# A planned attention and expert kernel: one attention pair joined at the start, one visit joined at the end, two constants of the planner changed

## The chip, the cores and the metric

The kernel runs on one core of a Trainium2 chip. The metric is device time in microseconds (us), from the start of an execution to its end. Before the change it takes 629.05 us, the median of three runs (628.59 to 629.12).

The core has five engines that matter here. TensorE (PE in the profile) multiplies matrices and writes to PSUM, which has eight banks. VectorE (DVE), ScalarE (ACT) and GpSimd (POOL) do elementwise work[...]. SyncE (SP) issues nearly all DMAs. Each engine takes its own instructions in order and waits on semaphores for the others.

## The reference

The first stage is a gated linear attention (4 sequences, 8 heads, 768 positions, head width 32, state width 16), taken in chunks. The second stage sends its result, as 3072 tokens of 256 numbers, through four expert layers and mixes them. All numbers are float32.

```python
for c in range(nc):                     # attention, chunk by chunk
    cum = np.cumsum(log_a[:, :, sl], axis=-1)
    M = einsum('bhin,bhjn->bhij', Cc, Bc) * exp(cum_i - cum_j) * causal
    y = einsum('bhij,bhjd->bhid', M, xc) + einsum('bhin,bhnd->bhid', Cc, state) * exp(cum)
    state = exp(sum(la)) * state + einsum('bhjn,bhjd->bhnd', Bc * exp(cum_last - cum), xc)
...
p = domain_probs / (domain_probs.sum(-1, keepdims=True) + 1e-09)
for e in range(E):                      # four experts, F = 1024
    h = np.maximum(x @ w1[e], 0.0)
    out += p[:, e:e + 1] * (h @ w2[e])
```

## The kernel before

**Tiling.** The kernel uses chunks of 128 positions, so there are 24 chunks: four sequences of six. The chunks are numbered so that the first four begin the four sequences and need no state from earlier. They are grouped in five blocks, of 4, 4, 4, 6 and 6 chunks, and a pair of chunks is 256 tokens. For the first three blocks (scheme B) and the last two (scheme H) the expert layers are computed with fast matrix multiplication: 7 products in place of 8 in scheme B, 15 in place of 18 in scheme H. The price is many sums of weights (L963), of tokens (L982), of hidden values (`combine`, L901) and of results (L1180). One product is two float32 matmuls of 128 x 128 by 128 x 256 (L874), and each of these shows as two records in the profile.

**Attention of a pair.** For each chunk, `decays` scans the decays into a buffer LT on VectorE (L496), makes a small product on GpSimd (`fade`, L506, into the buffer MT), and masks a copy of C on ScalarE (`mask`, L472). A visit of TensorE that computes scores (`score`, L479) fills four banks, and VectorE multiplies each with LT into MT (L798). A second visit (`outputs`) applies the state (L820, for chunks after the first four) and MT (L512, `inner`), and ScalarE copies the result out (L835), and the new state where there is a later chunk (L522). These visits use small tiles of the array, placed by `tile_position`. There are two MT buffers and one LT buffer.

**Opening.** Chunks 0 and 1 are written out by hand, up to 13.2 us. Chunks 2 and 3 come next, in `line`, TensorE's fixed order: the spreading of chunk 2's decays (L627), then scores and outputs of each chunk singly, with the first products of block 0 (`first`) between them. `beside` (L85) gives chunk 3 a second Value on the same LT and MT buffers, so that the planner sees no dependence between the two chunks there.

**The planner.** The program makes no schedule by hand after that. `Plan.add` records every job with the engines that may take it, its estimated time, what it needs and what it writes. `Plan.run` then plays the engines against each other and writes the instructions out in the order found. TensorE follows `line`. Every other engine takes, of the jobs that are ready and for which buffers are free, the one that is due first (`latest`). Three rules touch the change:

- A job that both VectorE and GpSimd may do (`B512`, `B256`: L901 without a PSUM operand, L963 for scheme B, L1180 without PSUM) is taken by GpSimd only if it will end in time there, and if VectorE has more urgent work that is ready, worth at least `BACK` us. The 100 sums of L963 for scheme H are for GpSimd alone.

```python
if max(ready, now) + w.on[e] > w.latest + late + SLACK or self.backlog(
        waiting["DVE"], now, t["DVE"], w) < BACK:
    continue
```

- Work on any engine but SyncE counts on the data of a load `MARGIN` us after the planned landing; the same holds for a buffer whose last user was a DMA.
- `PAIRS_AT` says, for a block of so many units followed by one of so many pairs, at which unit and place of `line` the next block's scores ("s0") and outputs ("o1", "o12") are visited. A unit is one group of fast products, some 26 us long (23 units in about 600 us). The key (6, 3) is that of block 3, in which the last block's attention is done.

Of the kernel before, what the change touches and what calls it, by code (L numbers as in the profile page):

```python
# [20 lines left out]
LANDING = 2.2  # L21
KEEP = 5
NV, NW = 31, 28
SLACK, BACK, YIELD = 0.0, 1.0, 6.0
EARLY = 1, 2, 3, 4, 5, 6, 7, 8, 9, 10
SOFT = 1
ROUND = 0, 3, 2, 0, 4
RATE, MARGIN = 330.0, 4.0
AFTER = 1
HOLD = 12.0  # L30
NEAR, WORTH, FIRST = .3, 1.0, 25.0
WAIT = .15
LANES, ISSUE = 8, .48
URGENT = {}
HELD = ("x", "w"), (5, 8), (0, 7)
LAST = (0, 1), (0, 2), (1, 1), (1, 2), (0, 0), (1, 0)
LATE = (13, 2), (6, 9), (11, 4), (10, 12), (3,), (1, 14), ("x", "w"), (5, 8), (0, 7)
# [6 lines left out]
}  # L44


# [5 lines left out]
class Value:  # L52
    def __init__(self, kind, seeded=False, fills=True):
        self.kind, self.seeded, self.fills = kind, seeded, fills
        self.home, self.writers, self.readers, self.left, self.end = None, [], [], 0, 0.0
        self.keeps = self.before = None

    @property
    def t(self):
# [12 lines left out]
class Plan:  # L72
# [9 lines left out]
        v.end = v.ready = ready  # L82
        return v

    def beside(self, v):  # L85

        u = Value(f"{v.kind} beside")
        u.home, u.end, u.ready = v.home, v.end, v.ready
        self.spare[u.kind] = []
        u.keeps = v  # L90
        return u

    def add(self, on, fn, reads=(), writes=(), part=(), lag=None, due=None, reuse=None, two=False,
            port=True, after=None, kb=0, hold=0.0, pieces=1):
        w = Work(on, fn, (.16 if "PE" in on else .09) if lag is None else lag)
        w.hold = hold
        w.two, w.port, w.after, w.kb, w.pieces = two, port, after, kb, pieces
        w.due, w.reuse = due, reuse
        w.ready = 0.0
        for v in reads:  # L100
            w.needs.update(v.writers)
            w.ready = max(w.ready, getattr(v, "ready", 0.0))
            v.readers.append(w)
        for v in writes:
            w.needs.update(v.writers)
            w.needs.update(v.readers)
            v.writers, v.readers = [w], []
        for v in part:
            w.needs.update(v.readers)
            v.writers = v.writers + [w]  # L110
        w.needs.discard(w)
        keeps = [v.keeps for v in (*reads, *writes, *part) if v.keeps]
        for v in dict.fromkeys([*reads, *writes, *part, *keeps]):
            w.touched.append(v)
            v.left += 1
        for n in w.needs:
            n.feeds.append(w)
        w.number = len(self.all)
        self.all.append(w)
        return w  # L120
# [222 lines left out]
def kernel(  # L343
# [15 lines left out]
    NSEQ = NCH // NC  # L359
# [65 lines left out]
    st = {c: {} for c in range(NCH)}  # L425
# [210 lines left out]
    LT, MT = ([homes[k][0][:, c] for c in range(2)] for k in ("LT", "MT"))  # L636
# [52 lines left out]
    ys = []  # L689
# [13 lines left out]
    plan = Plan(homes)  # L703
    line = []
    B512, B256 = {"DVE": D512, "POOL": 1.3}, {"DVE": D256, "POOL": .72}
    now = 13.2

    def pe(us, fn, **kw):
        w = plan.add({"PE": us}, fn, **kw)
        line.append(w)  # L710
        return w
# [22 lines left out]
        st[c]["xb"] = plan.taken("xb", i, now)  # L734
    st[2]["ctm"] = plan.taken("ctm", 0, now)
    st[3]["ab"] = plan.taken("ab", 0, now + 2)
    for k, i in (("LT", 0), ("MT", 1)):
        st[2][k] = plan.taken(k, i, now)
        st[3][k] = plan.beside(st[2][k])
    for c in range(2):  # L740
        st[c]["A"] = plan.taken("A", c, now)
    g0 = gates[0, 0] = plan.taken("gate", 0, now)
# [15 lines left out]
    def decays(c):  # L758
        s = st[c]
        j = c % 2  # L760
        for k in ("LT", "MT") if not j and "MT" not in s else ():
            s[k] = st[c + 1][k] = value(k)
        for part in range(2):
            if c < SPREAD:
                dve(1.2, lambda e, part=part: scan_quarters(
                    c, s["LT"].t[:, j], [b.t for b in s["a"]], part), reads=s["a"][2 * part:2 * part + 2],
                    part=[s["LT"]])
            else:
                half = NH * P // 2
                dve(1.15, lambda e, lo=half * part: scan(  # L770
                    s["LT"].t[:, j], s["ab"].t[:, lo:lo + half], place(c, lo // P) * P), two=True, reads=[s["ab"]], part=[s["LT"]])
        if c < NCH - NSEQ:
            plan.add({"POOL": .5 if place(c, 0) else .4}, lambda e: fade(c, s["MT"].t[:, j], s["xb"].t, s["LT"].t[:, j]),
                     reads=[s["xb"], s["LT"]], part=[s["MT"]])
        if "ctm" not in s:
            s["ctm"] = value("ctm")
            act(.62, lambda e: mask(c, s["ctm"].t, s["xb"].t), reads=[s["xb"]], writes=[s["ctm"]])
        if c >= NSEQ:
            s["dec"], s["cts"] = value("dec"), value("cts")
            dve(D256, lambda e: nc.vector.tensor_tensor_scan(  # L780
                out=s["dec"].t, data0=s["ah"].t, data1=zeros, initial=1.0,
                op0=ALU.mult, op1=ALU.add), two=True, reads=[s["ah"]], writes=[s["dec"]])
            plan.add({"POOL": .72}, lambda e: nc.gpsimd.tensor_mul(  # L783
                s["cts"].t, s["ctm"].t, s["dec"].t.unsqueeze(1).to_broadcast([HN, NT, P])),
                reads=[s["ctm"], s["dec"]], writes=[s["cts"]])

    def scores(cs):
        gs_ = [value("bank", fills=len(cs) == 2) for _ in range(NQ)]
        ss = [st[c] for c in cs]
        pe(.66 * len(cs), lambda e: score(  # L790
            cs, [s["ctm"].t for s in ss], [s["xb"].t for s in ss], [b.t for b in gs_]),
            reads=[s[k] for s in ss for k in ("ctm", "xb")], writes=gs_)
        s = ss[0]
        for r in (3, 2, 0, 1):
            def fn(e, r=r):
                g = gs_[r].t.rearrange("p (c t s) -> p c t s", c=2, t=NT)[:, :len(cs)]
                js, h = slice(cs[0] % 2, cs[0] % 2 + len(cs)), quarter(cs[0], r)
                nc.vector.tensor_mul(s["MT"].t[:, js, h, 0:P], g, s["LT"].t[:, js, h])  # L798

            dve(D512 if len(cs) > 1 else D256, fn, reads=[gs_[r], s["LT"]], part=[s["MT"]], hold=HOLD)  # L800
# [5 lines left out]
    def outputs(cs):  # L806
        ys = {c: value("bank", fills=False) for c in cs}
        for c in cs:
            if pair_of(c) not in yT:
                yT[pair_of(c)] = value("V")  # L810
        reads = [st[c][k] for c in cs for k in ("xb", "MT", "cts") if k in st[c]]
        reads += [S[c - NSEQ] for c in cs if c >= NSEQ]

        def fn(e):
            vs = {}
            for c in cs:
                vs[c] = v = ys[c].t[:, :NT * (P + N)].rearrange("p (t s) -> p t s", t=NT)
                for r in range(NQ) if c >= NSEQ else ():
                    rows, to = slice(32 * r, 32 * r + 32), 32 * ((r + turn_of(c)) % NQ)
                    nc.tensor.matmul(  # L820
                        out=v[to:to + 32, :, 0:P], lhsT=S[c - NSEQ].t[rows],
                        rhs=st[c]["cts"].t[rows], start=True, stop=False,
                        tile_position=(32 * r, to), skip_group_check=True)
            for c in cs:
                for t in range(NT):
                    inner(c, t, vs[c][:, t], st[c]["xb"].t, st[c]["MT"].t[:, c % 2],
                          P + N if c < NCH - NSEQ else P, c < NSEQ and t == 0)

        pe(.93 + .49 * len(cs) if cs[0] >= NSEQ else .75 * len(cs), fn, reads=reads, writes=list(ys.values()))
        for c in cs:  # L830
            s, y = st[c], ys[c]
            yt = yT[pair_of(c)]
            v = lambda y: y.t[:, :NT * (P + N)].rearrange("p (t s) -> p t s", t=NT)
            lo = c % 2 * P
            act(.28, lambda e, y=y, yt=yt, lo=lo: nc.scalar.copy(  # L835
                out=yt.t[:, :, lo:lo + P], in_=v(y)[:, :, 0:P]), reads=[y], part=[yt])
            if c < NCH - NSEQ:
                s["A"] = value("A")
                act((.1, .4, .2, .4)[turn_of(c)], lambda e, c=c, s=s, y=y: keep_state(
                    c, s["A"].t, v(y)[:, :, P:]), reads=[y], part=[s["A"]])  # L840
# [433 lines left out]
    fbs = range(EPB)  # L1274
# [11 lines left out]
    for fb in fbs:  # L1286
        first[fb, 0], h[fb, 0] = plain_first(0, fb, 0)
    decays(2)
    line.extend(first[0, 0])
    scores([2])  # L1290
    line.extend(first[1, 0])
    decays(3)
    outputs([2])
    scores([3])
    line.extend(first[2, 0])
    line.extend(first[3, 0])
    outputs([3])
    line.extend(visit(0, (2, 4), plain_terms(0, fbs, h, [(0, 0), (1, 0)])))
    for c in range(4):
        carry(c)  # L1300
# [146 lines left out]
```

## Time and profile before

| | before |
|---|---|
| median of 3 runs | 629.05 us |
| the profiled execution | 628.72 us |
| its span, first to last instruction | 626.9 us |
| granted TensorE clock | 1.000 |
| TensorE matmul / weight loads busy | 620.4 / 529.6 us |
| VectorE busy | 522.7 us, 822 instructions |
| ScalarE busy | 267.6 us, 563 instructions |
| GpSimd busy | 235.6 us, 257 instructions |
| DMA | 125.87 MB, mean 201 GB/s |

Busy time of TensorE is no measure here, since matmuls overlap in the pipeline and their ends are modelled; the distance from one matmul's start to the next one's is. A group's row gives the number of instructions, the time in which any of them ran, the mean of one, and the engine's idle time just before them with what ended it. The chain that ended last is followed back from the last instruction, at each step to what released it.

### The profile page before, as it was taken

What the parts mean: (1) busy time and instruction counts of PE and PEld (TensorE: products, weight loads), DVE (VectorE), ACT (ScalarE), POOL (GpSimd) and SP (SyncE); (2) the same over time, 40 slices, a digit from 0 to 9 for tenths busy, and PEclk for the clock granted to TensorE, in tenths of its full rate; (3) what the DMA queues carried; (4) which work ended last, traced back from release to release, by engine and by line L of the source; (5) the groups of instructions that cost most, each with busy time, mean ns of one, the idle gap of its engine ahead of it and who ended that gap; (6) DMA issues with size and microseconds to landing.
All of it is one profiled execution on the core that took longest, in us unless ns stands there. A gap on an engine that the chain in (4) does not pass through costs nothing.

```text
span 626.9 us, 10322 instructions
## 1 busy us (share of the span) xinstructions
PE 620.4 (99%) x3443; PEld 529.6 (84%) x3443; DVE 522.7 (83%) x822; ACT 267.6 (43%) x563; POOL 235.6 (38%) x257
## 2 busy tenths in 40 slices
PE   9999999999999999999999999999999999999997
PEld 5888888888888888888888888888888888888886
DVE  6989999988857799799779988959796967879684
ACT  4322553434355253246524335355444334554441
POOL 4244555662635756155763413220122310112020
PEclk9999999999999999999999999999999999999999
DMA  7989586673799875799999736636222229643001
GB/s 258 313 282 348 185 273 215 228 236 94 240 331 298 270 227 168 203 349 312 351 326 302 235 96 206 198 112 194 61 88 72 55 61 352 189 140 112 1 1 50
DMA packets 111733, 125.87 MB, mean 201 GB/s; under 512 B 28853, under 2 KB 78273, under 8 KB 111681
## 3 DMA queue, kind: packets, MB, share of 16 engines
q1 hardware_dynamic: 111412, 125.07, 62.6%
q8 instruction: 27, 0.44, 0.3%
q14 instruction: 26, 0.20, 0.1%
q10 hardware_dynamic: 268, 0.16, 0.1%
HBM read 100.30 MB, written 24.89 MB: 200 GB/s over the span
## 4 chain that ended last, share of the span: by engine, by line
PE 91%; DVE 7%; issue 1%; ACT 1%; DVEq 0%; ACTq 0%
PE bank L874 85%; PE bank L479 2%; PE bank L512 2%; DVE v L901 2%; DVE v L909 1%; DVE w L963 1%; DVE LT L496 1%; PE bank L651 1%; PE bank L820 1%; PE bank L627 1%; DVE dec L780 0%; DVE Y L982 0%; DVE MT L798 0%; PE bank L1252 0%; ACT A L522 0%
## 5 line engine op out<-in xcount | busy, mean ns | idle before, releaser
L874 PE MATMUL bank<-v,w 128*128 128x256 f32 x1864 | 438.9, 380 | 0.9 <-DVE v L901 0.7
L874 PEld LDWEIGHTS bank<-v,w 128*128 128x128 f32 x1864 | 352.4, 190 | 54.4 <-issue 3.9
L874 PE MATMUL bank<-Y,w 128*128 128x256 f32 x792 | 203.0, 379 | 0.7 <-ACT bank L888 0.7
L901 DVE TENSOR_TENSOR v<-v,v 128x512 f32<-128x512 f32 x219 | 178.4, 844 | 21.0 <-ACT v L883 19.5
L874 PEld LDWEIGHTS bank<-Y,w 128*128 128x128 f32 x792 | 150.4, 190 | 21.7 <-ACT bank L888 1.1
L901 POOL TENSOR_TENSOR v<-v,v 128x512 f32<-128x512 f32 x51 | 72.1, 1417 | 219.3 <-DVE v L909 124.1
L909 DVE SCALAR_TENSOR_TENSOR v<-bank,gate 128x512 f32<-128x512 f32 x172 | 116.7, 683 | 43.5 <-PE bank L874 39.1
L888 ACT COPY bank<-v 128x512 f32<-128x512 f32 (+1 forms) x192 | 108.3, 576 | 67.7 <-DVE v L901 46.2
L963 POOL TENSOR_TENSOR w<-w,w 128x256 f32<-128x256 f32 x106 | 96.9, 932 | 58.3 <-PE bank L874 35.0
L1129 ACT COPY v<-bank 128x512 f32<-128x512 f32 x107 | 62.6, 585 | 131.4 <-PE bank L874 129.5
L883 ACT COPY v<-bank 128x512 f32<-128x512 f32 x106 | 61.9, 584 | 102.0 <-PE bank L874 92.9
L496 DVE TENSOR_TENSOR_SCAN LT<-ab,ident 128x512 f32<-128x512 f32 x42 | 53.1, 1281 | 0.0
L901 DVE TENSOR_TENSOR v<-bank,v 128x512 f32<-128x512 f32 x40 | 27.4, 685 | 9.6 <-PE bank L874 9.5
L506 POOL TENSOR_TENSOR MT<-xb,LT 128x64 f32<-128x64 f32 (+1 forms) x28 | 15.3, 552 | 35.6 <-DVE LT L496 31.6
L798 DVE TENSOR_TENSOR MT<-bank,LT 128x512 f32<-128x512 f32 (+1 forms) x48 | 27.8, 632 | 0.9 <-PE bank L479 0.8
L1180 POOL TENSOR_TENSOR v<-v,v 128x256 f32<-128x256 f32 x18 | 17.2, 967 | 26.1 <-DVE v L1180 19.8
L783 POOL TENSOR_TENSOR cts<-ctm,dec 128x256 f32<-128x256 f32 x20 | 16.4, 825 | 14.1 <-ACT ctm L472 10.3
L1180 DVE TENSOR_TENSOR v<-v,v 128x256 f32<-128x256 f32 x42 | 17.4, 445 | 4.4 <-ACT v L1129 4.3
L1034 DVE TENSOR_TENSOR bank<-bank,v 128x512 f32<-128x512 f32 x22 | 15.3, 694 | 6.2 <-PE bank L874 6.0
L472 ACT ACTIVATE ctm<-xb,tmask 128x128 f32<-128x128 f32 x48 | 16.4, 395 | 4.1 <-DMA xb<-in_xbc_dram 2.1
L963 DVE TENSOR_TENSOR w<-w,w 128x256 f32<-128x256 f32 x32 | 16.5, 547 | 0.0
L963 POOL TENSOR_TENSOR w<-w 128x256 f32<-128x256 f32 x13 | 12.3, 944 | 10.4 <-PE bank L874 7.4
(72 smaller groups left out, 211.8 us busy)
## 6 DMA issues: line engine op xcount, KB each, us to landing
w<-in_w_dram SPq DMA_DIRECT2D x130, 256.0 KB
w<-w_d SPq DMA_DIRECT2D x130, 256.0 KB
w_d<-w SPq DMA_DIRECT2D x82, 256.0 KB
ab<-acut_d SPq DMA_DIRECT2D x21, 512.0 KB
w<-in_w_dram SPq DMA_DIRECT2D x38, 128.0 KB
gate<-p_d SPq DMA_DIRECT2D x10, 384.0 KB
xb<-in_xbc_dram SPq DMA_DIRECT2D x17, 192.0 KB
gate<-p_d SPq DMA_DIRECT2D x11, 256.0 KB
```

The costliest lines, as they stand in the source:

```text
L472: nc.scalar.mul(ctm[:, t], xb[:, OCT:OCT + P], tmask[:, t:t + 1])
L496: nc.vector.tensor_tensor_scan(out=LT.rearrange("p h s -> p (h s)")[:, lo:lo + w], data0=src, data1=ident.rearrange("p h s -> p (h s)")[:, ...
L783: plan.add({"POOL": .72}, lambda e: nc.gpsimd.tensor_mul(s["cts"].t, s["ctm"].t, s["dec"].t.unsqueeze(1).to_broadcast([HN, NT, P])), reads ...
L798: nc.vector.tensor_mul(s["MT"].t[:, js, h, 0:P], g, s["LT"].t[:, js, h])
L874: nc.tensor.matmul(out=o, lhsT=w[:, j], rhs=x if half is None else x[:, j], start=(start and j == 0), stop=(j == 1), skip_group_check=True)
L883: act(.5, lambda e: nc.scalar.copy(out=flat(v), in_=bank.t), reads=[bank], writes=[v])
L888: act(.54 if to > FB else .32, lambda e: nc.scalar.copy(out=bank.t[:, :to], in_=flat(v)[:, :to]), reads=[v], writes=[bank])
L901: plan.add(engines, lambda e: (on(e).tensor_add if sign > 0 else on(e).tensor_sub)(flat(v), whole(x), whole(y)), reads=[x, y], writes=[v], ...
L909: dve(D512, lambda e: nc.vector.scalar_tensor_tensor(out=h.t, in0=whole(x).rearrange("p (j m) -> p j m", j=JJ), scalar=0.0, in1=g.t[:, 2 * ...
L963: plan.add({"POOL": .72} if due else B256, lambda e, r=r, x=x, y=y, sign=sign: (on(e).tensor_add if sign > 0 else on(e).tensor_sub)(view(r ...
L1129: act(.5, lambda e: nc.scalar.copy(out=flat(v), in_=bank.t), reads=[bank], writes=[v])
L1180: plan.add(engines, lambda e: (on(e).tensor_add if sign > 0 else on(e).tensor_sub)(o[1](), x[1](), y[1]()), reads=[v for v in vs if v is n ...
```

## The change

There are four edits. The third and fourth chunk's scores are computed in one visit and their outputs in one visit; `beside` goes, and both chunks share a Value for LT and one for MT, as later pairs do. `SCORED = 4` puts the scores after the first four products of block 0. In the last block, the outputs of the second and third pair are computed in one visit, at the third pair's place, instead of each at its own. `BACK` goes from 1.0 to 3.0 us, and `MARGIN` from 4.0 to 2.0 us. The estimate of the planner for an outputs visit of the first four chunks is changed along with it.

```diff
-SLACK, BACK, YIELD = 0.0, 1.0, 6.0
+SLACK, BACK, YIELD = 0.0, 3.0, 6.0
...
-RATE, MARGIN = 330.0, 4.0
+RATE, MARGIN = 330.0, 2.0
...
+SCORED = 4
...
-    (6, 3): ((0, 1, "s0"), (0, 14, "o0"), (2, 1, "s1"), (2, 14, "o1"), (3, 1, "s2"), (3, 14, "o2")),
+    (6, 3): ((0, 1, "s0"), (0, 14, "o0"), (2, 1, "s1"), (3, 1, "s2"), (3, 14, "o12")),
...
-    for k, i in (("LT", 0), ("MT", 1)):
-        st[2][k] = plan.taken(k, i, now)
-        st[3][k] = plan.beside(st[2][k])
...
-        for k in ("LT", "MT") if not j and "MT" not in s else ():
+        for k in ("LT", "MT") if not j else ():
...
-        pe(.93 + .49 * len(cs) if cs[0] >= NSEQ else .75 * len(cs), fn, reads=reads, writes=list(ys.values()))
+        pe(.93 + .49 * len(cs) if cs[0] >= NSEQ else .4 + .49 * len(cs), fn, reads=reads, writes=list(ys.values()))
...
     decays(2)
-    line.extend(first[0, 0])
-    scores([2])
-    line.extend(first[1, 0])
     decays(3)
-    outputs([2])
-    scores([3])
-    line.extend(first[2, 0])
-    line.extend(first[3, 0])
-    outputs([3])
+    begun = [x for fb in fbs for x in first[fb, 0]]
+    line.extend(begun[:SCORED])
+    scores([2, 3])
+    line.extend(begun[SCORED:])
+    outputs([2, 3])
```

The rest of the diff removes `beside`, its field `keeps` and the lines in `Plan.add` that served it.

More of the change, by code (lines that the diff above doesn't have):

```diff
@@ L55, in __init__ @@
         self.home, self.writers, self.readers, self.left, self.end = None, [], [], 0, 0.0
-        self.keeps = self.before = None
+        self.before = None
     @property
@@ L83, in taken @@
         return v
[L85 to L91, printed above, removed]
     def add(self, on, fn, reads=(), writes=(), part=(), lag=None, due=None, reuse=None, two=False,
@@ L111, in add @@
         w.needs.discard(w)
-        keeps = [v.keeps for v in (*reads, *writes, *part) if v.keeps]
-        for v in dict.fromkeys([*reads, *writes, *part, *keeps]):
+        for v in dict.fromkeys([*reads, *writes, *part]):
             w.touched.append(v)
```

## The prediction

> **What bounds the kernel now.** I read the page's totals and its chain first, then the chain in order of time, then TensorE's timeline of the opening, then busy time by stage, then the groups. The totals, and the chain's shares by engine:
>
> ```profile
> PE 620.4 (99%) x3443; PEld 529.6 (84%) x3443; DVE 522.7 (83%) x822; ACT 267.6 (43%) x563; POOL 235.6 (38%) x257
> ...
> PE 91%; DVE 7%; issue 1%; ACT 1%; DVEq 0%; ACTq 0%
> ```
>
> TensorE carries 91% of the chain, VectorE 7%. Where these shares change is seen in the chain in order of time (start, us, what):
>
> ```profile
> 59.63 1.07 PE bank L874 x4
> 60.71 0.03 issue
> ...
> 79.45 0.61 DVE v L909
> ...
> 80.14 0.60 ACT bank L888
> 80.74 0.04 issue
> 80.78 16.68 PE bank L874 x76
> ...
> 280.14 0.64 PE bank L820 x32
> 280.79 2.14 PE bank L512 x64
> ...
> 387.77 0.59 PE bank L820 x16
> 388.36 1.01 PE bank L512 x32
> ...
> 418.35 199.63 PE bank L874 x924
> ```
>
> The last line gives TensorE's pace: 199.63 / 924 = 0.216 us from one big matmul to the next. With that pace I went through all 2656 starts of L874: outside the attention visits (L479, L820, L512) the pace breaks only three times, at 79.67 (1.109 us instead of 0.216), 108.30 (0.633) and 299.99 (1.047). That is 0.89 + 0.42 + 0.83, less the 0.10 that a restart costs anyway: 1.9 us of stall in all. Before the first two, the chain has run on VectorE (60.7 to 79.5, and 97.5 to 108.9). The rest of the span is work at full pace, 13.2 us of opening by hand, and about 9 us after the last dense stretch ends at 617.97. So a gain can only come from fewer or cheaper attention visits and from these 1.9 us.
>
> The opening, TensorE's timeline (start, us, engine, line, operation, tiles, shape, count):
>
> ```profile
> 15.13 0.71 PE L479 MATMUL bank<-ctm,xb 32*128 32x256 f32 x8
> 15.77 1.99 PE L874 MATMUL bank<-v,w 128*128 128x256 f32 x8
> 17.70 0.80 PE L512 MATMUL bank<-MT,xb 128*32 128x144 f32 x16
> 18.42 0.71 PE L479 MATMUL bank<-ctm,xb 32*128 32x256 f32 x8
> 19.07 3.72 PE L874 MATMUL bank<-v,w 128*128 128x256 f32 x16
> 22.72 0.70 PE L512 MATMUL bank<-MT,xb 128*32 128x144 f32 x16
> 23.34 14.94 PE L874 MATMUL bank<-v,w 128*128 128x256 f32 x68
> 38.22 1.15 PE L479 MATMUL bank<-ctm,xb 32*128 32x256 f32 x16
> ```
>
> To see here: each of the four visits is short, and a pair's scores (x16, from 38.22 to 39.29) take 1.07 us where two singles take 0.64 + 0.65.
>
> Busy time by stage (stretch, its length, PE, PEld, DVE, ACT, POOL, then clock and DMA):
>
> ```profile
> 50.00:75.00 25.00, 25.00 (x210) 20.98 (x209) 24.69 (x38) 10.11 (x22) 13.10 (x15) 1.00 0.73 249
> ```
>
> The two largest groups that either engine may take (busy us, mean ns, idle before and what ended it):
>
> ```profile
> L901 DVE TENSOR_TENSOR v<-v,v 128x512 f32<-128x512 f32 x219 | 178.4, 844 | 21.0 <-ACT v L883 19.5
> ...
> L901 POOL TENSOR_TENSOR v<-v,v 128x512 f32<-128x512 f32 x51 | 72.1, 1417 | 219.3 <-DVE v L909 124.1
> ```
>
> VectorE is full from about 40 to 110 us (24.69 of 25), and there alone it limits TensorE. In 400 to 425 it is busy 17.89 of 25.
>
> **What the Trainium skill says.** "Perfetto Trace Analysis", Identifying the Most-Contended Engine: matmul busy time is a poor measure of a full TensorE, weight-load time a better one. Agreed: I use start to start (0.216 us) and not the 99%; weight loads stand at 84%. "TensorEngine Tiling (Array Packing)", Key Properties: changing the tiling mode drains TensorE. The trace agrees: the big matmul before a visit takes 0.309 us to the next start, the first after it 0.320, against 0.216: 0.20 us for each visit. "SBUF — State Buffer", Who interferes with whom: an operation of VectorE with two inputs in SBUF and one of GpSimd that reads SBUF shut each other out. The trace agrees: of the 219 operations in the DVE row above, 125 with no GpSimd operation beside them took 683 ns (0.603 from start to start), 94 with one took 1059 ns.
>
> **The change part by part.**
>
> *The opening.* Today: 0.64 + 0.72 + 0.65 + 0.62 us for four visits, and six changes between visit and dense work (two visits adjoin) at 0.10: 3.2 us. After: the paired scores 1.07, paired outputs (32 of L512, 1.05, half of a visit with 64) and four changes: 2.5. That removes 0.7 us, if nothing is late. What may be late is MT on VectorE, which has no idle time there. The third chunk's scans end at 16.23. The fourth chunk's second mask ends at 17.00 on ScalarE; the paired scores come after 16 dense matmuls, at 16.75, and begin with the third chunk's half (0.35 us), so they wait about nothing. VectorE then has the two scans of the fourth chunk (2.33 us), which now share one buffer with the third's and so are planned after its small GpSimd product (16.71); one gate product (0.60) fits in before. Four products of 0.60 follow: 16.23 + 0.60 + 2.33 + 2.40 = 21.56, against 21.48 when TensorE arrives. Stall 0.1; without the gate product, none. The remaining three or four gate products (0.60 each) feed a visit from 22.6 that eats one per 0.43 us; the last is needed at 23.9 and done near 23.5. Gain **0.6 us**, from 0.7 down to 0 if VectorE is one scan later. VectorE itself saves 8 x 0.331 - 4 x 0.60 = 0.25 us. Loads and their queue keep their order here.
>
> *The last block's two pairs in one visit.* One pair costs 389.30 - 387.39 = 1.91 from the last dense start before to the first after, less 0.216 of it, plus 0.10: 1.80 us; two, 3.60. A joint one: 0.64 + 2 x 1.01 + 0.20 = 2.86 (last-block shape; the joint visit at 280.14 took 2.78 with the wider one). Gain **0.7 us**. It needs four free banks at once, and ScalarE copies four tiles out in about 2.0 us instead of 1.0. VectorE is idle a quarter of the time there and the result is used only two units later, so I take nothing off; if banks lack, up to one copy, 0.6 us.
>
> *BACK from 1 to 3.* Jobs that GpSimd may take: on it now 51 of L901, 19 of L1180, and of L963 19 (the code has 64 sums open to both engines, VectorE ran 45). A moved L901 adds 0.60 us to VectorE, a moved half-size one 0.335; each us of GpSimd work that goes relieves VectorE by about 0.20 (the stretching of L901, L963, L780 and L496 beside GpSimd sums to 46 us, over 235.6). If half move: 25 x 0.60 + 19 x 0.335 - 54 x 0.20 = **+10 us of VectorE**, covered by VectorE's idle time after 110 (some 93 of its 104 us); zero on the path. Uncovered it is only in 40 to 110: there at most 2 of L901 and 12 sums, 2 x 0.60 + 12 x 0.335 = 5.2 us if all move and nothing is relieved. From the other side, near 299 two L901 on GpSimd (295.10 and 297.23) stretch a scan to 1.68 and a sum to 1.15 right ahead of the third stall: without them up to 0.8 comes back, and in all at most 1.9. I take **0**.
>
> *MARGIN from 4 to 2.* It removes no work; compute engines are planned up to 2 us sooner after a load. VectorE waited for DMA only in the first 4 us (1.1). GpSimd did wait for loads ("DMA w<-in_w_dram 5.5" in three places), so planned landings are already early when DMA is busy. 2 us more of that on GpSimd is covered (it is idle 62%); on VectorE between 40 and 110 each would cost up to 2. The scores in the opening do not go through it. I take **0**, from -0.5 to +2.
>
> Sum: -0.6 - 0.7 = **-1.3 us** on a span of 626.9: 625.6. That execution took 628.72, 1.8 more than its span; the median is 629.05, so the forecast is 629.05 - 1.3 = **627.7**.
>
> **Rivals.**
>
> 1. *The stalls go as well* (less shutting out by GpSimd): -1.3 and up to -1.9, 625.8 to 626.9. For it: the stretched operations ahead of all three stalls. Against: most GpSimd work at 60 to 110 is sums for later blocks that only GpSimd may do, and it stays.
> 2. *VectorE becomes the bound for longer*: in the gapless stretch from 40 to 110, jobs that GpSimd took with a backlog of 1 to 3 us now queue on VectorE, or VectorE waits for a load. The stalls near 80 and 108 grow by up to 5.2 from the sums, 2 from a load. It decides from 2.6 us of added VectorE time there (1.3 to eat the gain, 1.26 to be seen): 630.3 to 632.9. For it: there is no slack, 0.3 us of idle. Against: relief, and a backlog there may be above 3 anyway.
> 3. *The opening's gain is given back* at 79.7, as VectorE needs the same time to get there: 628.3 to 628.9. Against: it waited for TensorE at 32.3, 34.0 and 39.4 (3.3 us), so an earlier TensorE moves it too.
> 4. *The threshold hardly binds*, GpSimd keeps its share: the same -1.3, within the forecast.
>
> **How the numbers follow.** The forecast, with rival 4, has 0.40 (626.9 to 628.7); rival 1, 0.20; rival 3, 0.08; rival 2, 0.32. A plan is laid anew by two constants, and a list of orders has more ways to get worse than the 1.9 us it can recover, hence the weight of rival 2. 0.2% is 1.26 us, about what a measurement here can tell: faster is below 627.8, slower above 630.3. The forecast's case straddles the first: 0.22 faster, 0.18 same. Faster 0.42, same 0.26, slower 0.32. The range leaves out the lowest quarter of rival 1 and the upper third of rival 2: 626.0 to 631.8; the likeliest case alone is 626.9 to 628.7.
>
> **What would show it.** Right: two visits fewer between 13 and 24, the dense work after them starting at 22.6 to 22.8; one visit with 32 of L820 near 416 and none near 388; GpSimd's L901 about 25; the pace of 0.216 unbroken but near 80, 108 and 300. Wrong: new breaks of pace from 40 to 110 behind VectorE (rival 2), VectorE waiting for a load, or a break at the four-bank visit.

## The result, and the profile after

The changed kernel takes 625.18 us, the median of four runs (624.95 to 625.32), against 629.09 us before in the same session: the ratio is 0.9938, with a 95% interval of 0.9921 to 0.9956. It is 3.9 us faster, where 1.3 us was forecast, and lies below the range of 626.0 to 631.8. The profiled executions took 625.31 us (span 623.5) and 628.72 us (span 626.9), so the two traces differ by 3.4 us, and that is what they can account for. Lines of the changed kernel have other numbers: L874 is now L863, L901 is L890, L909 is L898, L963 is L952, L1180 is L1169, L496 is L488, L798 is L787, L479 is L471, L512 is L504, L820 is L809.

The page after, totals and the chain's shares by engine:

```profile
PE 618.5 (99%) x3443; PEld 530.0 (85%) x3443; DVE 525.2 (84%) x889; ACT 267.7 (43%) x563; POOL 141.8 (23%) x186
...
PE 97%; DVE 1%; issue 1%; ACT 0%; DVEq 0%
```

TensorE's share of the chain rose from 91% to 97%, VectorE's fell from 7% to 1%. GpSimd does 94 us less, and VectorE, which took that work, is busy only 2.5 us longer. The chain in order of time (start, us, what), after:

```profile
16.22 0.58 DVE v L898
16.81 2.25 DVE LT L488 x2
19.05 0.06 DVE v L898
19.11 0.44 issue
19.55 2.49 DVE MT L787 x4
22.04 0.04 issue
22.08 1.18 PE bank L504 x30
...
59.48 11.42 PE bank L863 x52
...
73.66 37.32 PE bank L863 x172
110.98 1.08 PE bank L471 x16
...
281.29 37.32 PE bank L863 x172
...
412.40 0.64 PE bank L809 x32
413.04 1.90 PE bank L504 x64
414.94 199.63 PE bank L863 x924
```

From 73.66 to 110.98, and from 281.29 to 318.61, TensorE runs 172 matmuls without a break; before, these stretches held the breaks at 79.67, 108.30 and 299.99. Near 388 there is no visit any more, and the one at 412 serves both pairs. The opening, TensorE's timeline after:

```profile
16.86 1.15 PE L471 MATMUL bank<-ctm,xb 32*128 32x256 f32 x16
17.93 3.72 PE L863 MATMUL bank<-v,w 128*128 128x256 f32 x16
21.58 1.68 PE L504 MATMUL bank<-MT,xb 128*32 128x144 f32 x32
23.19 14.94 PE L863 MATMUL bank<-v,w 128*128 128x256 f32 x68
```

The outputs visit lasts 1.61 us from start to start instead of the forecast 1.05; the dense work after it starts 0.15 us earlier than before, not 0.6. Taken at equal places of TensorE's order, the 3.40 us lie here:

| where | before | after | won |
|---|---|---|---|
| dense work after the third and fourth chunk's outputs | 23.34 | 23.19 | 0.15 |
| dense work after the scores near 112 (breaks at 79.67, 108.30) | 113.66 | 111.98 | 1.53 |
| dense work after the scores near 320 (break at 299.99) | 322.16 | 319.62 | 0.86 |
| dense work after the last outputs (416 before, 412 after) | 418.27 | 414.87 | 0.86 |

So the two joint visits gave 0.15 + 0.86 = 1.01 us, and the breaks that went 1.53 + 0.86 = 2.39 us. The tail is the same: 8.96 us from 617.97 to the end before, 8.96 from 614.57 after.

For the experiments I use one measure: from the first big matmul's start to the last one's. It leaves out the opening by hand, whose length varies by 0.7 us between profiles. It is 608.28 us before (13.20 to 621.48) and 604.88 after. The breaks before cost 0.89 + 0.42 + 0.83 and, since a restart costs 0.10 more, 2.45 us in all; the changed kernel lost 0.55 us in its opening. Without any loss the old structure would take 605.83 us and the new one 604.33. So 1.50 us are structure and 1.90 us are losses that went away; the 0.55 us that the changed kernel loses in its opening counts against the losses here (2.45 - 0.55), and against the joint visits in the 1.01 above. "Loss" below is what a kernel takes over its structure's figure. It is read from one profiled execution of each kernel, so the ratio beside it, from all executions, counts for more: with BACK = 3.5 the profiled execution (627.38 us) was the fastest of twelve, whose median is 628.56.

### The profile page after: what moved, and what is told of

Read it like the earlier page. It is cut to its first block, busy times and chain, and to the rows that moved or that the text cites. A ratio compares the mean times of both kernels' runs of the same rounds, so it can differ in the third digit from the quotient of the medians.

```text
span 623.5 us, 10234 instructions
## 1 busy us (share of the span) xinstructions
PE 618.5 (99%) x3443; PEld 530.0 (85%) x3443; DVE 525.2 (84%) x889; ACT 267.7 (43%) x563; POOL 141.8 (23%) x186
## 4 chain that ended last, share of the span: by engine, by line
PE 97%; DVE 1%; issue 1%; ACT 0%; DVEq 0%
PE bank L863 91%; PE bank L504 2%; PE bank L471 2%; DVE LT L488 1%; PE bank L643 1%; PE bank L809 1%; PE bank L619 0%; DVE MT L787 0%; PE bank L1241 0%; PE bank L611 0%; ACT A L514 0%; DVE v L898 0%; ACT v L686 0%; DVE v L1169 0%; DVE v L1246 0%
## 5 line engine op out<-in xcount | busy, mean ns | idle before, releaser
L863 PE MATMUL bank<-v,w 128*128 128x256 f32 x1864 | 438.1, 380 | 0.0
L863 PEld LDWEIGHTS bank<-v,w 128*128 128x128 f32 x1864 | 352.5, 190 | 52.5 <-issue 3.1
L863 PE MATMUL bank<-Y,w 128*128 128x256 f32 x792 | 202.9, 379 | 0.0
L890 DVE TENSOR_TENSOR v<-v,v 128x512 f32<-128x512 f32 x261 | 185.2, 740 | 20.3 <-ACT v L872 19.0
L863 PEld LDWEIGHTS bank<-Y,w 128*128 128x128 f32 x792 | 150.4, 190 | 20.6 <-issue 0.2
L898 DVE SCALAR_TENSOR_TENSOR v<-bank,gate 128x512 f32<-128x512 f32 x172 | 116.8, 684 | 35.1 <-PE bank L863 29.6
L952 POOL TENSOR_TENSOR w<-w,w 128x256 f32<-128x256 f32 x94 | 82.5, 899 | 76.2 <-PE bank L863 44.1
L890 POOL TENSOR_TENSOR v<-v,v 128x512 f32<-128x512 f32 x9 | 12.8, 1419 | 236.7 <-DVE v L890 183.3
L488 DVE TENSOR_TENSOR_SCAN LT<-ab,ident 128x512 f32<-128x512 f32 x42 | 51.2, 1228 | 0.0
L890 DVE TENSOR_TENSOR v<-bank,v 128x512 f32<-128x512 f32 x40 | 27.5, 689 | 8.8 <-PE bank L863 8.4
L787 DVE TENSOR_TENSOR MT<-bank,LT 128x512 f32<-128x512 f32 x44 | 27.7, 678 | 0.6 <-PE bank L471 0.6
L1169 DVE TENSOR_TENSOR v<-v,v 128x256 f32<-128x256 f32 x57 | 22.5, 427 | 4.8 <-ACT v L1118 4.7
L498 POOL TENSOR_TENSOR MT<-xb,LT 128x64 f32<-128x64 f32 (+1 forms) x28 | 11.6, 420 | 50.5 <-DVE LT L488 33.1
L464 ACT ACTIVATE ctm<-xb,tmask 128x128 f32<-128x128 f32 x48 | 16.2, 394 | 11.8 <-DMA xb<-in_xbc_dram 10.4
L952 DVE TENSOR_TENSOR w<-w,w 128x256 f32<-128x256 f32 x44 | 18.2, 443 | 0.6 <-issue 0.4
L952 POOL TENSOR_TENSOR w<-w 128x256 f32<-128x256 f32 x12 | 9.5, 792 | 33.1 <-DMA w<-in_w_dram 19.0
L1121 ACT COPY v<-bank 128x256 f32<-128x256 f32 x18 | 6.7, 372 | 19.9 <-PE bank L863 19.7
```

The costliest lines, as they stand in the source:

```text
L464: nc.scalar.mul(ctm[:, t], xb[:, OCT:OCT + P], tmask[:, t:t + 1])
L488: nc.vector.tensor_tensor_scan(out=LT.rearrange("p h s -> p (h s)")[:, lo:lo + w], data0=src, data1=ident.rearrange("p h s -> p (h s)")[:, ...
L863: nc.tensor.matmul(out=o, lhsT=w[:, j], rhs=x if half is None else x[:, j], start=(start and j == 0), stop=(j == 1), skip_group_check=True)
L890: plan.add(engines, lambda e: (on(e).tensor_add if sign > 0 else on(e).tensor_sub)(flat(v), whole(x), whole(y)), reads=[x, y], writes=[v], ...
L898: dve(D512, lambda e: nc.vector.scalar_tensor_tensor(out=h.t, in0=whole(x).rearrange("p (j m) -> p j m", j=JJ), scalar=0.0, in1=g.t[:, 2 * ...
L952: plan.add({"POOL": .72} if due else B256, lambda e, r=r, x=x, y=y, sign=sign: (on(e).tensor_add if sign > 0 else on(e).tensor_sub)(view(r ...
```

## The experiments

**Which constant, and is it the engine or the plan?** The theory after the result was A: jobs that leave GpSimd relieve VectorE, and so the breaks go. Its rivals were B, that MARGIN did it, and C, that breaks are accidents of one plan. Four kernels, on one chip. First BACK alone, in the kernel before:

```diff
-SLACK, BACK, YIELD = 0.0, 1.0, 6.0
+SLACK, BACK, YIELD = 0.0, 3.0, 6.0
```

> The kernel before with BACK = 3 alone. Theory A (less GpSimd work beside VectorE relieves VectorE, and so the three breaks of TensorE's pace go): GpSimd's L901 falls from 51 to about 10, VectorE's busy time rises by less than 5 us, the 2.4 us of breaks (0.89 + 0.42 + 0.83 and 0.10 for each restart) go: about 626.7 us. Theory B (MARGIN did it, since data count sooner): the same shift of jobs, breaks of 2 us or more remain: 629 us or more. Theory C (the breaks are accidents of one plan, and any new plan has others): breaks at new places, 0 to 4 us.

Measured: ratio 0.9992 (0.9984 to 1.0001), no gain that can be told. GpSimd's L901 fell to 9 and VectorE's busy time rose by 7.7 us, yet the loss is still 2.04 us: a break at 79.68 and a wait in the visit near 174.

```diff
-RATE, MARGIN = 330.0, 4.0
+RATE, MARGIN = 330.0, 2.0
```

> The kernel before with MARGIN = 2 alone. Theory A: GpSimd's L901 stays near 51 and breaks of pace of 2 to 3 us remain: 628.5 to 629.5 us. Theory B: the breaks go: about 626.7 us. Theory C: breaks at new places, 0 to 4 us.

Measured: 0.9986 (0.9980 to 0.9993), loss 1.63 us: 627.95 us at the median, where B expected about 626.7, with breaks at 90.5 and 197.4, where none were. A and B both fall as single causes. The next kernel has both structural edits and the constants of before (the changed kernel with the two diffs above taken back):

> The changed kernel with BACK = 1 and MARGIN = 4 as before, so the two structural edits alone. All theories: the joint visit near 416 saves 0.85 us and the opening 0.15, as in the changed kernel. Theory A: breaks of about 2.4 us remain where VectorE is full, so 628.1 us. Theory C: breaks anywhere, 626 to 630.

Measured: 1.0002 (0.9994 to 1.0010). The last outputs visit cost 2.74 us, as in the changed kernel, but there are five breaks (2.49 us in all), four of them where the kernel before has none and one, at 80.29, behind the same matmul as the break at 79.67 before; and the scores of the opening waited. Loss 3.89 us: the structure's 1.50 us are there, and all of it was lost again. Last, the old plan, with only the engine of the shared jobs changed:

```diff
     for w in done:
-        w.fn(w.by)
+        w.fn("DVE" if len(w.on) > 1 else w.by)
```

> The plan of the kernel before, job for job and in the same order, but each of the 89 jobs that it gave to GpSimd and that VectorE may do is written out for VectorE at its place; TensorE's, ScalarE's and SyncE's orders are the same. No new plan is made, so only the engine differs. Theory A: relief nearly pays for the added jobs, VectorE's busy time rises by less than 5 us, breaks of pace fall to 1 us or less: 626.7 to 627.7 us. Theories B and C: VectorE has 89 jobs more than the plan gave it (about 45 us by 0.603 and 0.335 each), breaks grow: 630 us or more.

Measured: 1.0038 (1.0025 to 1.0051). The group of sums on VectorE in this kernel (busy us, mean ns, idle before), to be held against the row with x219 in the prediction (178.4 us, 844 ns):

```profile
L901 DVE TENSOR_TENSOR v<-v,v 128x512 f32<-128x512 f32 x270 | 190.2, 734 | 20.0 <-ACT v L883 18.9
```

51 more sums cost 11.8 us, 0.23 each instead of 0.60, because all others get shorter (844 to 734 ns). In all, VectorE is busy 12.6 us longer for 51 x 0.603 + 38 x 0.335 = 43.5 us of work. Still the loss grows from 2.45 to 4.88 us: relief pays for most of the added work over the whole span (some 31 of 43.5 us), not at the places where VectorE is late. Theory A falls.

**The two constants crossed with the structure.** Both constants in the kernel before (the two one-line diffs above together):

> The kernel before with BACK = 3 and MARGIN = 2, the structure as before. The two constants alone left breaks of pace (waits inside visits counted) of 1.9 us (BACK) and 1.4 us (MARGIN) instead of 2.1. Theory D (the two constants together, whatever the structure, give a plan that keeps VectorE's jobs in time): no breaks, 2.1 us and their restarts gone: span near 624.6 us, time near 626.7. Theory C (which breaks a plan has is an accident of its order): breaks of 1 to 3 us at some places, time 627.5 to 629.5.

The changed kernel with BACK = 1:

> The changed kernel with BACK = 1 as before, MARGIN = 2. Theory D: about 1.4 us of breaks come back, as with MARGIN alone in the old structure: 626.6 to 627.2 us. Theory C: breaks of 0 to 4 us at other places than in any kernel so far. If BACK does nothing: none, 625.2 us.

The changed kernel with MARGIN = 4:

> The changed kernel with MARGIN = 4 as before, BACK = 3. Theory D: about 1.9 us of breaks come back: 627.0 to 627.5 us. Theory C: 0 to 4 us at other places. If MARGIN does nothing: none, 625.2 us.

Measured: 0.9972 (0.9961 to 0.9982), 0.9999 (0.9989 to 1.0009) and 0.9977 (0.9969 to 0.9985). With the kernels above, this fills a table of losses in us:

| BACK, MARGIN | old structure | new structure |
|---|---|---|
| 1, 4 | 2.45 (before) | 3.89 |
| 3, 4 | 2.04 | 2.58 |
| 1, 2 | 1.63 | 3.86 |
| 3, 2 | 1.29 | 0.55 (after) |

Nothing adds up here. Each constant lowers the loss in the old structure, BACK by no more than its runs can tell; in the new one MARGIN alone does nothing and both together take off 3.3 us. Theory D, in its strict form (no breaks with both constants, whatever the structure), is wrong: the old structure keeps the breaks near 79 and 108.

**The third break.** In the old plan, only the two L901 that GpSimd ran right ahead of the break at 299.99 go to VectorE:

```diff
+    shared = [w for w in done if w.by == "POOL" and w.on.get("DVE") == D512][14:16]
     for w in done:
-        w.fn(w.by)
+        w.fn("DVE" if w in shared else w.by)
```

> The plan of the kernel before, with only the two L901 that GpSimd ran at 295.10 and 297.23 written out for VectorE at their places. The relief theory, kept for this place alone: the scan at 298.2 (1.68 us) falls to 1.21 and the sums beside them from 1.1 to 0.68, which is 0.47 + 0.43 + 0.47 us less for 1.21 us more, so the break at 300 (0.83) shrinks little or not at all: within 0.3 us of before. If the load on VectorE decides: the break grows by up to 1.2 us. If the lock of the shared read interface decides: it goes, 0.9 us less.

Measured: 1.0005 (0.9997 to 1.0014), no change of the time that can be told. In its profile the stretched sum did fall to 0.68 us, but the break grew from 0.83 to 1.46 us. The scan at 298.7 was still stretched, to 1.76 us, now with the product L783 beside it (start, us, engine, line, operation, tiles, shape, count):

```profile
298.17 1.25 POOL L783 TENSOR_TENSOR cts<-ctm,dec 128x256 f32<-128x256 f32 x1
298.74 1.76 DVE L496 TENSOR_TENSOR_SCAN LT<-ab,ident 128x512 f32<-128x512 f32 x1
```

So the prediction's bound for this place, up to 0.8 us back, had the wrong sign in this profile.

**What makes VectorE late.** Of GpSimd's work near the breaks, most is weight sums that it alone may do. Here they keep their place in the plan and write the same bytes, but read nothing, which leaves the sums out:

```diff
-                plan.add({"POOL": .72} if due else B256, lambda e, r=r, x=x, y=y, sign=sign: (
+                plan.add({"POOL": .72} if due else B256, lambda e, r=r, x=x, y=y, sign=sign, due=due: nc.gpsimd.memset(view(r), 0.0) if due else (
                     on(e).tensor_add if sign > 0 else on(e).tensor_sub)(view(r), view(x), view(y)),
```

> The plan of the kernel before, job for job, but the 100 weight sums of scheme H that only GpSimd may do are written as a fill of the same output with zeros, which reads nothing (it leaves these sums out). VectorE's, TensorE's, ScalarE's and SyncE's orders are the same. Theory E (VectorE is late near 80, 108 and 300 because operations of GpSimd that read SBUF stretch it, these sums above all): VectorE's busy time falls by 10 us or more, the breaks at 79.7 and 108.3 (1.5 us with restarts) go and that at 300 shrinks: 626.5 to 627.5 us. Rival (VectorE's own jobs and what they wait for are too many there, GpSimd beside it matters little): breaks of 2 us or more remain, 628.5 to 629 us.

Measured: 0.9971 (0.9962 to 0.9981). Busy time from 60 to 110 us (stretch, its length, PE, PEld, DVE, ACT, POOL, clock and DMA), in the kernel before, in this one, and in the changed kernel:

```profile
60.00:110.00 50.00, 49.02 (x309) 41.96 (x308) 48.62 (x80) 24.24 (x56) 27.59 (x27) 1.00 0.68 225
```

```profile
60.00:110.00 50.00, 50.00 (x316) 43.48 (x315) 44.18 (x82) 24.60 (x57) 14.68 (x30) 1.00 0.75 249
```

```profile
60.00:110.00 50.00, 50.00 (x316) 43.45 (x315) 48.13 (x88) 25.20 (x58) 22.84 (x27) 1.00 0.73 242
```

VectorE does two operations more in 4.4 us less, and TensorE is busy through; over the whole span VectorE's busy time falls from 522.7 to 502.1 us. The chain of this kernel has no VectorE there:

```profile
59.63 11.42 PE bank L874 x52
71.05 0.64 PE bank L820 x32
71.69 2.11 PE bank L512 x64
73.81 37.32 PE bank L874 x172
```

The breaks at 79.67 and 108.30 are gone, the one at 300 is left (0.79). There the two L901 on GpSimd remain, and the scan beside them still takes 1.68 us. The fills are also shorter (310 ns against some 930) and waited for loads 0.6 us in all, but in the list of waits of before no wait of VectorE for GpSimd reaches 1 us, so what the sums do to VectorE there is to stretch it. Shown, then, for the old plan: the first two breaks exist because operations of GpSimd that read SBUF, the scheme H sums above all, stretch VectorE where it is full. This is what "SBUF — State Buffer", Who interferes with whom, says of two-input operations, which contend with GpSimd instructions that read SBUF and not with those that only write it. The trace agrees: of the 219 sums L901 with both inputs in SBUF, 146 with nothing of GpSimd beside them took 683 ns, 11 with only a fill beside them 681, and 62 with a reading operation beside them 1040.

For all kernels I summed, over VectorE's instructions that start from 60 to 110 us, what each took beyond the lower quartile of its own kind (times set so that the first big matmul starts at 13.20 in every kernel):

| kernel | stretching, us | breaks of pace in 60 to 110 |
|---|---|---|
| fills for sums | 3.6 | none |
| changed, NEAR = 1.0 (two runs) | 5.4, 5.9 | none |
| changed (two runs) | 5.7, 5.6 | none |
| changed, MARGIN = 1.5 | 6.8 | none |
| changed, MARGIN = 2.5 | 7.1 | one |
| before, forced to VectorE | 7.5 | two |
| before, BACK = 3 | 7.7 | one |
| changed, BACK = 2.5; changed, MARGIN = 4; before, both | 8.1 each | three; two; two |
| changed, BACK = 3.5 | 8.8 | one |
| before, MARGIN = 2; before | 9.8; 9.9 | one; two |
| changed, BACK = 1; before, two moved; changed, old constants | 10.2; 10.4; 10.5 | two; two; three |

The line falls between 6.8 and 7.1 us. It was drawn after the fact and is thin: with a start at 62 us in place of 60, the kernel with MARGIN = 1.5, without a break, has 6.7 us, and that with 2.5, which has one, 6.0. So more stretching goes with breaks, but no threshold is shown. The changed kernel does 88 operations there, before 80, in about the same busy time. Above the line, the size of the breaks doesn't follow the stretching; that it hangs on which job is stretched is argued, not shown. GpSimd ran 20 of L963 and two of L901 there before, 18 and one in the changed kernel; with 27 instructions in both, it is busy 22.84 us instead of 27.59. How long it is busy doesn't decide alone: the operations that it starts there take 28.0 us with MARGIN = 1.5, without a break, and 23.8 with 2.5, which has one. What is left is which operations meet, that is the order; no run tests this by itself.

**Region or one order?** Four neighbours of the changed kernel:

> The changed kernel with BACK = 3.5. Theory D (BACK and MARGIN are good in a region around 3 and 2): breaks of pace and waits in visits of 0.6 us or less, 625.0 to 625.7 us. Theory C (the changed kernel's plan without breaks is one lucky order among many): 1 to 3 us of breaks at some places in 50 to 180 us, 626 to 628 us. GpSimd's share hardly differs (one job less).

> The changed kernel with MARGIN = 2.5. Theory D: breaks and waits of 0.6 us or less, 625.0 to 625.7 us. Theory C: 1 to 3 us of breaks at some places in 50 to 180 us, 626 to 628 us.

> The changed kernel with BACK = 2.5. Theory D (region): breaks and waits of 0.6 us or less, 625.0 to 625.7 us. Theory C (one order among many): 1 to 3 us of breaks, 626 to 628 us.

> The changed kernel with MARGIN = 1.5. Theory D: breaks and waits of 0.6 us or less, 625.0 to 625.7 us. Theory C: 1 to 3 us of breaks, 626 to 628 us.

Measured, as ratios to before on the same chip: 1.0003 (0.9994 to 1.0011), 0.9971 (0.9960 to 0.9982), 1.0008 (0.9994 to 1.0021), 0.9942 (0.9928 to 0.9955). In their profiles the losses are 2.62, 2.05, 4.75 and 0.82 us, the first with breaks at 375.6 and 403.5, where no other kernel has one. One of four is as good as the changed kernel. Theory C holds better than D, though not in the form that breaks come at ever new places. Every kernel here has the same 2656 big matmuls in the same order. Counted along it, the place of the break at 79.67 has one in nine of the 16 kernels, that of 108.30 in six: two tight places, and the plan decides whether they break. The place of 299.99 has one only in the four kernels that keep the old plan's order (before, the two that move jobs to VectorE, and the fills); every new plan is without it, and what in the old order made it stays open. For the constants: half a us in BACK gives an order that is some 4 us worse (either way, by the medians), half a us in MARGIN one that is some 1.5 us worse (2.5) or as good (1.5). On average the new structure's five orders near (3, 2) lose 2.2 us, its two with BACK = 1 lose 3.9, so there is a tendency, too weak to count on (one profile each).

**The opening.** Two small transposes of states stood ahead of the third chunk's scans. With a longer NEAR they come after:

```diff
-NEAR, WORTH, FIRST = .3, 1.0, 25.0
+NEAR, WORTH, FIRST = 1.0, 1.0, 25.0
```

> The changed kernel with NEAR = 1.0 instead of 0.3: in the first 25 us VectorE may wait up to 1 us for a more urgent job. Nothing moves but two small transposes of states, which now come after the scans and products of the third and fourth chunk; the other engines' orders are the same. In the changed kernel the first scan waited behind the first transpose until 13.83, though its data were there at about 13.3. If that is what made the joint outputs late (TensorE waited 0.5 us before 22.08): the wait falls to 0.1 or less and stays won to the end, 624.7 us. If the later full stretch of VectorE gives it back: 625.2.

Measured: 0.9957 (0.9944 to 0.9970), with executions from 624.93 to 627.04. The profile did what was expected, a loss of 0.12 us instead of 0.55, but the median was 626.06. So it ran once more beside the changed kernel itself:

> The changed kernel itself, beside the others of this call: 625.2 us, no break of pace.

> The changed kernel with NEAR = 1.0. If the 0.43 us that its first profile shows as won in the opening stay won: 0.3 to 0.5 us below the changed kernel of this call. If its executions differ because VectorE sometimes waits longer for a load (1.33 us near 108 in the first profile, hidden there): between 0.5 below and 1.5 above, and a slower execution's profile has a break near 108.

Measured: the changed kernel 625.33 us (ratio 0.9945, 0.9931 to 0.9958), this one 625.41 (0.9945, 0.9932 to 0.9957): no difference that can be told. In its second profile the outputs waited for nothing, but the scores visit, with the changes before and after it, took 1.62 us instead of 1.27, so that only 0.14 us was won. What holds the scores up is seen best in the changed kernel with the old constants, where that visit took 2.06; its chain:

```profile
6.36 5.37 DMA acut_d<-a_cut
...
11.79 5.06 DMA ab<-acut_d
...
16.88 0.35 ACTq L589
...
17.64 0.40 ACT ctm L464
...
18.08 0.71 PE bank L471 x8
```

The decays go out to memory and back in two transfers; ScalarE's issue of another store (L589) comes after the second, and the fourth chunk's mask stands behind that issue. No experiment slowed an execution down on purpose, so why this kernel's spans vary by 2.1 us stays open; its two profiles are of executions of 624.93 and 625.41 us.

## Why the prediction was wrong

*Direction and range.* Faster was right, in part by luck: the two joint visits on which the forecast rested show no gain with the old constants (1.0002), since that plan lost what they won. That the new constants would make a better plan was not in the forecast. The size was off by a factor of three. The event was the first rival's, to which 0.20 was given, and even its range (625.8 to 626.9) began above the result, mainly because the three breaks were counted as 1.9 us. The 0.10 of each restart was taken off where it had to be added: the first matmul after each break took 0.320 us to the next start instead of 0.216, so the breaks cost 2.45.

*The opening, 0.6: measured 0.15.* The failing term is "one gate product fits in before". The planner put a second one (18.97 to 19.55) between the fourth chunk's scans and the four products, so MT was ready at 22.03 instead of 21.56 and TensorE waited 0.5 us. The other terms stood, nearly: 1.07 for the paired scores, 2.25 for the scans, 2.49 for the products; the outputs visit takes 1.12 us where nothing waits, not 1.05. "They wait about nothing" held in this profile (1.27, with its changes), not in others (1.62 and 2.06), as the fourth mask waits on a chain of transfers.

*The last block's visit, 0.7: measured 0.86.* The joint visit took 2.74 us instead of 2.86. Four banks at once cost nothing.

*BACK.* "If half move" was low: 71 of 89 jobs moved (42 of 51 L901, 16 of 19 L1180, 13 of 19 sums). Relief "about 0.20" per us was low as well: 42 x 0.603 + 29 x 0.335 = 35.0 us of work raised VectorE's busy time by 2.5 us, and 0.25 was saved in the opening, so GpSimd's 94 us less gave back some 32 us, or 0.34 per us, if the whole difference is put down to it; forcing the old plan gave 0.29. But this isn't why the breaks went, as the forced plan shows.

*BACK and MARGIN on the path, "I take 0": measured -2.4* (1.53 + 0.86 in the table of places). This is the step that failed. The sum treated a constant of the planner as moving jobs within a plan that stays. It makes another plan, and the price of that lies not at 0 but in a band: over all kernels here, losses run from 0.1 to 4.9 us over the structure, with before at 2.45. The argument against the first rival, that GpSimd's own sums stay and so the shutting out stays, was half right: at 79.67 and 108.30 they are the cause, as the fills show, and they stayed, but the stretching from 60 to 110 us fell from 9.9 to 5.7 us. That this is so because they meet other operations is argued from the comparison of plans; why this order meets fewer can't be read from the profile of before. The second rival, slower by VectorE's load, did not occur in this kernel; it did in the forced one. Its "0.3 us of idle" is that of 50 to 75 us alone: from 40 to 110 VectorE was busy 68.30 of 70.

*The fourth rival,* that the threshold hardly binds, is refuted by GpSimd's group after:

```profile
L890 POOL TENSOR_TENSOR v<-v,v 128x512 f32<-128x512 f32 x9 | 12.8, 1419 | 236.7 <-DVE v L890 183.3
```

## What to carry to other kernels

Split a change to a planned kernel into what it removes from the bound engine's order (here 1.0 us, or 1.5 without a wait of its own, with 1.3 forecast) and what a new plan does to the losses; price the second as a band, from plans near the old one, and never as 0. Where VectorE is full, count the GpSimd operations that read SBUF beside it, whoever owns them: with the sums read no more, the breaks there went, and over all plans more stretching went with breaks, while moving the shared jobs alone made things worse. A constant that wins by one order is to be tried anew after every edit: the old constants in the new structure lost all that the structure won.

## What was not expected of the hardware

How much executions of one program differ is not the same from plan to plan: on one chip 626.78 to 626.85 us in six with MARGIN = 2.5 and 627.38 to 630.35 in twelve with BACK = 3.5, on another 627.51 to 633.07 in twelve with BACK = 2.5. The two longest of the last, 631.29 and 633.07, had a granted clock of 0.996 and 0.994, the others 0.998 or more and at most 629.75; whether the clock made them long is not shown, and there is no profile of either. It is not the whole reason: with NEAR = 1.0, executions of 624.93 and 627.04 both had 1.000. Waits for loads are another candidate. In the profile with BACK = 2.5 (629.24 us) VectorE waits for loads up to 63.7 (0.82 us), 208.7 (1.22) and 558.7 (1.02), before only in the first 4 us. That such waits make the spread is not shown either: with MARGIN = 1.5 two of them last 2.0 us each (up to 206.6 and 275.5), and its four executions lie within 1.0 us.
